# Gated attention and a mixture of experts in one kernel: the early load of the first expert's tokens one slot sooner

## The chip, the cores and the metric

The kernel runs on one core of one Trainium2 chip. A core has five engines, each with an instruction stream of its own that runs strictly in order: TensorE (PE), VectorE (DVE), ScalarE (ACT), GpSimd (POOL) and SyncE (SP), which issues most transfers. The metric is the time on the device in microseconds (us), the median of several runs. The profiled execution has a span of 387.1 us, from its first to its last instruction.

## The reference: what is computed

```python
f = 1.0 / (1.0 + np.exp(-f_logit))                    # B, H, S, D = 4, 8, 768, 48
for t in range(S):                                    # gated linear attention
    state = f[:, :, t, :, None] * state + np.einsum('bhd,bhe->bhde', k[:, :, t], v[:, :, t])
    y[:, :, t] = np.einsum('bhd,bhde->bhe', q[:, :, t], state)
x = y.transpose(0, 2, 1, 3).reshape(3072, 384)        # one row per token
logits = x @ w_gate                                   # 8 experts
expert_idx = np.argmax(logits, axis=1)                # one expert per token
# gate_w: the softmax's value at that expert; each expert takes at most `capacity` tokens, in order
h = np.maximum(disp @ w1, 0.0)                        # (rows, 384) x (384, 1024)
out = gate_w * (h @ w2)                               # (rows, 1024) x (1024, 384), back to the token's row
```

## The kernel before

**Attention** runs in chunks of 128 tokens: 24 chunks (`NT`), 6 to a batch. A loop over `slots`, 0 to 24, writes out by hand the order of the instructions on all five engines; work of neighbouring chunks is interleaved in a slot. In slot n TensorE does, in this order: `keys_pe(n)` (transposes, L443), `scores_pe(n + 1)` (L418), `kq_in(n + 2)` (transposes, L358), `inter(n)` (query times state, L460), `update(n)` (L480), the ranks of a group of tokens (`rank_pe`, L667 to L674), `rows_pe(n - 1)` (the finished token rows, L535) and `values(n)` (L514). Between them stand `early_job(n, 0)`, `early_job(n, 1)` and `early_job(n, 2)`: before `inter`, after it, and after `values`.

**Choice of the expert.** Token rows go into a ring of 12 chunks. For the five groups of chunks that end before chunk 18, `choose_sum`, `choose_max` and `choose_first` find each token's expert on VectorE with help of GpSimd, `rank` and `put` give each token its row in the DRAM buffer `disp`, and the chunks join `queue`. `flush_scatter` takes one chunk from it and stores its 128 rows by index into `disp` (GpSimd, L318). `SCATTERS` says how many are taken in slot n behind `carry(n)` (2 where it has no entry); from slot 20 on `rows_copy` takes one more.

**Weights of the first expert** come in seven pieces (`PIECE_LOAD`: the slot of the load). ScalarE rounds each piece (`split_high`, in the slot of `PIECE_SPLIT`) and a second engine subtracts (`split_low`, L143): VectorE for pieces 3 to 6, GpSimd for pieces 0 to 2, in four parts each. `QUARTERS` gives the slot, the piece and the number of parts there.

**The early part of the first expert.** Its first 256 tokens (`T_FIRST[0]`) are known when chunk 14 is stored (`SPLIT = 15`). One transfer brings them from `disp` to `xg0` (L940). It is issued on SyncE behind slot 20 and waits for the store of chunk 14 (`early_ins`). `early_prep(c)` turns 128 columns of it (two transposes on TensorE, L710, then a rounding on ScalarE, L711, and a subtraction on VectorE, L712), `early_pe(ft)` is one of eight blocks of nine products (L745), and `early_out(ft)` takes a block out of its PSUM bank with one instruction on ScalarE (`hh`, L751) and one on VectorE (`hl`, L752). `EARLY` lists the slot and the place of each. The products of three pools (`psF`, `psT`, `psA`, two banks each) wait for a free bank.

**The experts** follow: `ffn2_rows` for the early tokens, then the rest of expert 0 and the seven others in order of size.

Of the kernel before, what the change touches and what calls it, by code (L numbers as in the profile page):

```python
# [14 lines left out]
ALU = mybir.AluOpType  # L15
# [4 lines left out]
P = 128  # L20
# [8 lines left out]
def kernel(  # L29
# [12 lines left out]
    nc = tc.nc  # L42
    B, H, S, D = q.shape
    N, DM = out.shape
    NE = w_gate.shape[1]
# [5 lines left out]
    NT = B * S // C  # L51
# [20 lines left out]
    PIECE_LOAD = (5, 8, 13, 17, 18, 21, 21)  # L72
    PIECE_SPLIT = (9, 11, 17, 20, 21, 22, 23)
    PARTS = 4
    QUARTERS = {9: (0, 1), 10: (0, 1), 11: (0, 2), 12: (1, 2), 15: (1, 2), 18: (2, 2), 21: (2, 2)}
    SCATTERS = {n: 1 for n in range(NT - 3)}
    PAD_ACT = 7

    const = ctx.enter_context(tc.tile_pool(name="const", bufs=1))
# [24 lines left out]
    def after(ins, other, why):  # L104
        if other is not None:
            tc.add_manual_dep(
                ins.ins,
                other.name,
                mybir.DependencyInfo(mybir.DependencyClass.Sync, mybir.DependencyReason.DATA),
                reason=why,  # L110
            )
# [80 lines left out]
    def load(nm, n):  # L192
        if n >= (NT // 2 if nm == "f" else NT):
            return
        t = loads[nm, n % NLOAD[nm]]
        if nm == "v":
            b, t0 = n // CPB, n % CPB * C
            nc.sync.dma_start(t[:, :, :D], srcs[nm][b, :, t0 : t0 + C, :].rearrange("h p d -> p h d"))
            return
        t = t.rearrange("t h j d -> t h (j d)")  # L200
        if nm == "kq":
            for h, x in enumerate(nm):
                nc.sync.dma_start(t[64 * h : 64 * h + 64], pairs(x, n, C))
        elif n == 0:
            for h, queue in enumerate((nc.sync, nc.scalar)):
                hs = slice(4 * h, 4 * h + 4)
                queue.dma_start(t[:64, hs], pairs(nm, 0, C)[:, hs])
        else:
            nc.sync.dma_start(t, pairs(nm, 2 * n, 2 * C))
# [51 lines left out]
    desc = const.tile([P, NE], F32, name="desc")  # L261
# [301 lines left out]
    def group(g, m):  # L563
        c = g % RING
        return ring_parts[:, c : c + m], rows_at(g, m)[:, :, DM : DM + NE]
# [6 lines left out]
    def choose_max(g, m):  # L572
        part, L = group(g, m)
        most = abuf.tile([P, m], F32, name="r_m")
        nc.vector.tensor_reduce(out=most, in_=L, axis=AX.X, op=ALU.max)
        w = abuf.tile([P, m, NE], F32, name="r_w")
        nc.vector.tensor_tensor(w, L, most.unsqueeze(2).broadcast_to([P, m, NE]), op=ALU.is_equal)
        return w

    def choose_first(g, m, w):  # L580
        nc.gpsimd.tensor_tensor(w, w, desc.unsqueeze(1).broadcast_to([P, m, NE]), op=ALU.mult)
        wm = abuf.tile([P, m], F32, name="r_wm")
        nc.vector.tensor_reduce(out=wm, in_=w, axis=AX.X, op=ALU.max)
        oh = tallies[-1][:, 1 : m + 1]
        nc.vector.tensor_tensor(oh, w, wm.unsqueeze(2).broadcast_to([P, m, NE]), op=ALU.is_equal)
        chosen[g] = oh, m
# [92 lines left out]
    def flush_scatter():  # L679
        if queue:  # L680
            n = queue.pop(0)
            late = n >= SPLIT
            ins = scatter(disp, ri_of.pop(n), row_at(n), NV * RPE - 1, ("disp", "late") if late else ("disp",))
            if not late:
                early_ins[:] = [ins]
# [34 lines left out]
    def early_out(ft):  # L720
        hs0.append(hidden_out(ph0.pop(ft), T_FIRST[0], ft, h0pool, T_FIRST[0]))

    EARLY = {
        (NT - 2, 0): ((early_prep, 0),),
        (NT - 2, 1): ((early_prep, 1),),
        (NT - 2, 2): ((early_prep, 2),),
        (NT - 1, 0): ((early_pe, 0), (early_pe, 1)),
        (NT - 1, 1): ((early_out, 0), (early_pe, 2)),
        (NT - 1, 2): ((early_out, 1), (early_out, 2), (early_pe, 3), (early_pe, 4)),
        (NT, 0): ((early_out, 3), (early_pe, 5)),  # L730
        (NT, 1): ((early_out, 4),),
        (NT, 2): ((early_pe, 6), (early_pe, 7), (early_out, 5), (early_out, 6)),
    }

    def early_job(n, at):
# [81 lines left out]
    def slot(n):  # L817
# [16 lines left out]
        while half:  # L834
            choose_first(*half.pop())
# [45 lines left out]
        if nxt:  # L881
            for s in range(SCATTERS.get(n, 2)):
                flush_scatter()
# [11 lines left out]
        if fn and n >= PAD_ACT:  # L895
            kq_pad(n + 3)
            load("kq", n + 6)
        if n in QUARTERS:
            k, parts = QUARTERS[n]
            for part in range(parts):  # L900
# [9 lines left out]
        while full:  # L910
            g = full.pop()
            half.append((*g, choose_max(*g)))
        if prev and done and not tail:
            g, m = done
# [11 lines left out]
        if tail:  # L926
            early_job(n, 2)
            g, m = done
# [7 lines left out]
                split_low(pieces[k], nc.vector)  # L936
        if n == 4:
            nc.gpsimd.tensor_copy(cap, cap_i[:, 0:1])
        if n == NT - 4:
            ins = nc.sync.dma_start(xg0, dispv[0, : T_FIRST[0]].rearrange("(k p) w -> p k w", p=P))  # L940
            tc.declare_no_dep(ins.ins, group="late", reason="later tokens of this expert go to rows of their own")
            after(ins, early_ins[0], "the rows of the early tokens")
# [72 lines left out]
    with tc.manual_schedule(  # L1015
        engines={
            mybir.EngineType.PE,
            mybir.EngineType.Activation,
            mybir.EngineType.DVE,
            mybir.EngineType.Pool,  # L1020
            mybir.EngineType.SP,
        }
    ):
        prologue()
        for n in slots:
            slot(n)
        while queue:
            flush_scatter()
        early_out(7)
        g0 = gates(xg0, T_FIRST[0] // P, h0pool)  # L1030
# [392 lines left out]
```

## Time and profile before

| | us |
|---|---|
| median of 3 runs | 389.07 |
| lowest and highest | 388.64, 389.6 |
| the profiled execution's own time | 389.2 |
| its span | 387.1 |

The profiled execution lies 0.13 us above the median; 2.1 us of its own time lie outside its span. By the page TensorE is busy for 374.4 us (97%) of the span, VectorE 212.4 (55%), ScalarE 201.4 (52%) and GpSimd 178.5 (46%). A busy time of TensorE says nothing about its pace, since its clock is granted at one of two levels; the clock of a stretch is a column of its own. Times of rows count from the span's start. In the rows a releaser in brackets is what ended the idle time before the instruction.

### The profile page before, as it was taken

To read this page: it belongs to the slowest core of one execution; us is meant where nothing else is said; L and a number is where in the kernel's file an instruction comes from. 1 tells how busy PE (TensorE), PEld (TensorE's weight loads), DVE (VectorE), ACT (ScalarE), POOL (GpSimd) and SP (SyncE) were. 2 spreads that over 40 slices of the span, in tenths; PEclk is the share of its full clock that TensorE was granted. 3 is DMA by queue.
4 is the path that set the end of the run, shared out by engine and by line. 5 is a ranking of instruction groups with operands and counts; after the bars stand their busy time and mean duration, and the time that the engine had idled before them with its cause. 6 is when DMAs were issued, how large, how long until landed. Compare 5 with 4: busy or idle time off the path is not lost.

```text
span 387.1 us, 10152 instructions
## 1 busy us (share of the span) xinstructions
PE 374.4 (97%) x4009; PEld 350.6 (91%) x4009; DVE 212.4 (55%) x490; ACT 201.4 (52%) x425; POOL 178.5 (46%) x263
## 2 busy tenths in 40 slices
PE   8999999999997999999999999999999999999994
PEld 7999888899887789998899989999999999999993
DVE  4998898989989447553844343325235335232310
ACT  3466578877877322462835452544464464462311
POOL 6755546777675832436164340280280271292011
PEclk9999999999999699999999999999999999999999
DMA  8999999999962412669576083165056137211001
GB/s 157 176 207 211 239 251 233 243 225 248 243 154 83 164 68 103 224 206 322 165 253 209 5 270 119 43 218 197 36 179 195 61 108 228 73 58 42 14 23 40
DMA packets 83324, 60.88 MB, mean 157 GB/s; under 512 B 65671, under 2 KB 77829, under 8 KB 83268
## 3 DMA queue, kind: packets, MB, share of 16 engines
q1 hardware_dynamic: 79476, 50.13, 50.3%
q0 software_dynamic: 3520, 9.92, 7.1%
q8 instruction: 33, 0.54, 0.6%
q14 instruction: 23, 0.19, 0.2%
q10 hardware_dynamic: 272, 0.10, 0.1%
HBM read 49.42 MB, written 11.43 MB: 157 GB/s over the span
## 4 chain that ended last, share of the span: by engine, by line
PE 71%; issue 9%; DVE 8%; DMA 4%; POOL 4%; SPq 2%; ACT 1%; POOLq 1%; DVEq 0%
PE psM L1177 14%; PE psA L745 12%; PE psM L745 11%; PE psM L1006 9%; PE psA L418 3%; PE psA L535 3%; PE psY L514 2%; DMA ld_kq<-in_q_dram 2%; PE psT L1148 2%; DVE Rq L392 2%; DVE Suf L378 2%; PE psF L358 2%; PE psY L460 2%; PE psA L368 2%; PE psF L745 2%
## 5 line engine op out<-in xcount | busy, mean ns | idle before, releaser
L318 POOL DMA_INDIRECT out_dram<-yo,g_ti x30 | 30.0, 999 | 101.1 <-ACT yo L1193 40.3
L143 POOL TENSOR_TENSOR w2l<-raw,w2h 128x768 fp32r<-128x768 f32 x28 | 51.1, 1855 | 38.5 <-ACT w2h L134 27.8
L752 DVE SCALAR_TENSOR_TENSOR hl<-psA,hh 128x224 fp32r<-128x224 f32 (+8 forms) x33 | 18.4, 559 | 49.3 <-ACT hh L751 49.3
L143 DVE TENSOR_TENSOR w1l<-raw,w1h 128x1024 fp32r<-128x1024 f32 x21 | 25.4, 1220 | 23.2 <-ACT w1h L134 23.2
L1006 PE MATMUL psM<-w2h,hh 128*128 128x384 f32 (+2 forms) x112 | 37.6, 342 | 0.0
L1006 PE MATMUL psM<-w2l,hh 128*128 128x384 f32 (+2 forms) x112 | 37.5, 338 | 0.0
L1006 PE MATMUL psM<-w2h,hl 128*128 128x384 f32 (+2 forms) x112 | 37.4, 337 | 0.0
L134 ACT ACTIVATE w1h<-raw 128x1024 fp32r<-128x1024 f32 x24 | 25.3, 1062 | 23.1 <-DMA raw<-in_moe_w_dram 23.0
L752 DVE SCALAR_TENSOR_TENSOR hl<-psM,hh 128x224 fp32r<-128x224 f32 (+7 forms) x32 | 17.8, 563 | 31.3 <-ACT hh L751 31.3
L426 POOL TENSOR_SCALAR_AFFINE_SELECT AT<-AT 128x512 f32<-128x512 f32 x48 | 29.7, 643 | 10.1 <-ACT AT L424 9.8
L1177 PE MATMUL psM<-hh,w2h 128*128 128x440 f32 (+3 forms) x96 | 34.1, 355 | 0.0
L1177 PE MATMUL psM<-hl,w2h 128*128 128x440 f32 (+3 forms) x96 | 34.1, 355 | 0.0
L134 ACT ACTIVATE w2h<-raw 128x768 fp32r<-128x768 f32 x32 | 27.1, 846 | 13.3 <-DMA raw<-in_moe_w_dram 12.5
L1177 PE MATMUL psM<-hh,w2l 128*128 128x440 f32 (+3 forms) x96 | 33.8, 352 | 0.0
L318 POOL DMA_INDIRECT disp<-rows,ri x24 | 24.2, 1007 | 17.1 <-DVE tally L645 5.6
L378 DVE TENSOR_TENSOR_SCAN Suf<-psF,direv 112x511 f32<-112x511 f32 x24 | 29.1, 1211 | 4.1 <-PE psF L358 4.1
L751 ACT ACTIVATE hh<-psA 128x224 fp32r<-128x224 f32 (+8 forms) x33 | 16.2, 492 | 26.9 <-PE psA L745 26.2
L745 PE MATMUL psM<-xh,w1h 128*128 128x480 f32 (+6 forms) x84 | 29.8, 354 | 0.0
L745 PE MATMUL psM<-xl,w1h 128*128 128x480 f32 (+6 forms) x84 | 29.8, 354 | 0.0
L745 PE MATMUL psA<-xh,w1h 128*128 128x480 f32 (+6 forms) x84 | 29.7, 353 | 0.0
L745 PE MATMUL psA<-xh,w1l 128*128 128x480 f32 (+6 forms) x84 | 29.5, 351 | 0.0
L392 DVE TENSOR_TENSOR_SCAN Rq<-psF,d 112x512 f32<-112x512 f32 x24 | 29.4, 1224 | 0.0
(238 smaller groups left out, 969.3 us busy)
## 6 DMA issues: line engine op xcount, KB each, us to landing
raw<-in_moe_w_dram SPq DMA_DIRECT2D x24, 512.0 KB, 4.5
raw<-in_moe_w_dram SPq DMA_DIRECT2D x32, 384.0 KB, 3.5
ld_kq<-in_k_dram SPq DMA_DIRECT2D x24, 192.0 KB, 5.4
ld_kq<-in_q_dram SPq DMA_DIRECT2D x24, 192.0 KB, 5.2
ld_v<-in_v_dram SPq DMA_DIRECT2D x24, 192.0 KB, 4.0
ld_f<-in_f_logit_dram SPq DMA_DIRECT2D x11, 384.0 KB, 6.3
xg<-disp SPq DMA_DIRECT2D x6, 589.5 KB, 5.0
xg<-disp SPq DMA_DIRECT2D x3, 393.0 KB
```

The lines of the kernel that those rows point to most:

```text
L134: return nc.scalar.activation(hi, raw, AF.Copy)
L143: engine.tensor_tensor(lo[cs], raw[cs], hi[cs].bitcast(F32), op=ALU.subtract)
L318: ins = nc.gpsimd.indirect_dma_start(out=dst, out_offset=bass.IndirectOffsetOnAxis(ap=idx, axis=0), in_=rows, in_offset=None, bounds_check ...
L378: nc.vector.tensor_tensor_scan(out=_view(Suf[:R], m - 1, [[-1, m]]), data0=_view(F, m, [[-1, m]]), data1=_view(direv[:R], m - 1, [[-1, m]] ...
L392: nc.vector.tensor_tensor_scan(out=Rq[:R], data0=F, data1=d1[:R], initial=0.0, op0=ALU.mult, op1=ALU.max)
L418: nc.tensor.matmul(pas[s][:, p], kTs[n][r, p], qTs[n][r, p], start=True, stop=True)
L426: nc.gpsimd.affine_select(AT[:, s], AT[:, s], pattern=[[0, NP], [1, C]], compare_op=ALU.is_ge, fill=0.0, base=0, channel_multiplier=-1)
L745: nc.tensor.matmul(ph[:, :T], a[:, c, fs], x[:, c, :T], start=(n == 0), stop=(n == 3 * DT - 1))
L751: ins = nc.scalar.activation(hh[:, :T], ph[:, :T], AF.Relu).ins
L752: nc.vector.scalar_tensor_tensor(out=hl[:, :T], in0=ph[:, :T], scalar=0.0, in1=hh[:, :T].bitcast(F32), op0=ALU.max, op1=ALU.subtract)
L1006: nc.tensor.matmul(py[:n], x[:, ks], a[:, ft], start=(ft == 0 and m == 0), stop=(ft == FT - 1 and m == 2))
L1177: nc.tensor.matmul(pys[c][:, :T], a[:, ft, cs], x[:, :T], start=(ft == 0 and n == 0), stop=(ft == FT - 1 and n == 2))
```

## The change

Five things are edited. The transfer into `xg0` is issued behind slot 19 instead of slot 20 (`NT - 5`). `SCATTERS` takes two chunks in slots 18 and 19 and none in slot 20, so that chunk 14 is stored in slot 19. `EARLY` moves the transposes from slot 22 to slots 21, and the blocks of products from slots 23 and 24 to slots 22, 23 and 24. In `choose_max` VectorE multiplies by `desc`, which GpSimd did in `choose_first`. `QUARTERS` moves parts of the subtraction on GpSimd to other slots.

```diff
--- before.py
+++ after.py
@@ -72,8 +72,8 @@
     PIECE_LOAD = (5, 8, 13, 17, 18, 21, 21)
     PIECE_SPLIT = (9, 11, 17, 20, 21, 22, 23)
     PARTS = 4
-    QUARTERS = {9: (0, 1), 10: (0, 1), 11: (0, 2), 12: (1, 2), 15: (1, 2), 18: (2, 2), 21: (2, 2)}
-    SCATTERS = {n: 1 for n in range(NT - 3)}
+    QUARTERS = {11: (0, 3), 12: (0, 1), 15: (1, 3), 17: (1, 1), 20: (2, 2), 21: (2, 2)}
+    SCATTERS = {n: 2 if n in (18, 19) else 0 if n == 20 else 1 for n in range(NT - 3)}
     PAD_ACT = 7
 
     const = ctx.enter_context(tc.tile_pool(name="const", bufs=1))
@@ -575,10 +575,10 @@
         nc.vector.tensor_reduce(out=most, in_=L, axis=AX.X, op=ALU.max)
         w = abuf.tile([P, m, NE], F32, name="r_w")
         nc.vector.tensor_tensor(w, L, most.unsqueeze(2).broadcast_to([P, m, NE]), op=ALU.is_equal)
+        nc.vector.tensor_tensor(w, w, desc.unsqueeze(1).broadcast_to([P, m, NE]), op=ALU.mult)
         return w
 
     def choose_first(g, m, w):
-        nc.gpsimd.tensor_tensor(w, w, desc.unsqueeze(1).broadcast_to([P, m, NE]), op=ALU.mult)
         wm = abuf.tile([P, m], F32, name="r_wm")
         nc.vector.tensor_reduce(out=wm, in_=w, axis=AX.X, op=ALU.max)
         oh = tallies[-1][:, 1 : m + 1]
@@ -721,15 +721,16 @@
         hs0.append(hidden_out(ph0.pop(ft), T_FIRST[0], ft, h0pool, T_FIRST[0]))
 
     EARLY = {
-        (NT - 2, 0): ((early_prep, 0),),
-        (NT - 2, 1): ((early_prep, 1),),
-        (NT - 2, 2): ((early_prep, 2),),
-        (NT - 1, 0): ((early_pe, 0), (early_pe, 1)),
-        (NT - 1, 1): ((early_out, 0), (early_pe, 2)),
-        (NT - 1, 2): ((early_out, 1), (early_out, 2), (early_pe, 3), (early_pe, 4)),
-        (NT, 0): ((early_out, 3), (early_pe, 5)),
-        (NT, 1): ((early_out, 4),),
-        (NT, 2): ((early_pe, 6), (early_pe, 7), (early_out, 5), (early_out, 6)),
+        (NT - 3, 1): ((early_prep, 0),),
+        (NT - 3, 2): ((early_prep, 1), (early_prep, 2)),
+        (NT - 2, 0): ((early_pe, 0), (early_pe, 1)),
+        (NT - 2, 1): ((early_out, 0), (early_out, 1)),
+        (NT - 2, 2): ((early_pe, 2),),
+        (NT - 1, 0): ((early_out, 2), (early_pe, 3)),
+        (NT - 1, 1): ((early_out, 3), (early_pe, 4)),
+        (NT - 1, 2): ((early_out, 4), (early_pe, 5)),
+        (NT, 0): ((early_out, 5),),
+        (NT, 2): ((early_pe, 6), (early_pe, 7), (early_out, 6)),
     }
 
     def early_job(n, at):
@@ -936,7 +937,7 @@
                 split_low(pieces[k], nc.vector)
         if n == 4:
             nc.gpsimd.tensor_copy(cap, cap_i[:, 0:1])
-        if n == NT - 4:
+        if n == NT - 5:
             ins = nc.sync.dma_start(xg0, dispv[0, : T_FIRST[0]].rearrange("(k p) w -> p k w", p=P))
             tc.declare_no_dep(ins.ins, group="late", reason="later tokens of this expert go to rows of their own")
             after(ins, early_ins[0], "the rows of the early tokens")
```

How the instructions stand on TensorE around slots 21 and 22; `xg` is `xg0`, `x0h` and `x0l` are its turned halves, L746 is the old L745. A row with `x2` stands for two instructions.

```order
 L460 MATMUL psY<-qT,S_149 64x128
+L710 MATMUL psF<-ident,xg_85 128x128 x2
 L480 MATMUL psA<-ld_v_112,kn 64x48
...
 L514 MATMUL psY<-AT,ld_v_112 64x128
+L710 MATMUL psF<-ident,xg_85 128x128 x4
 L443 MATMUL psT<-ident,kT 128x64
...
 L418 MATMUL psA<-qT,kT 128x128 x8
-L710 MATMUL psF<-ident,xg_85 128x128 x2
+L746 MATMUL psF<-x0h,w1h 128x256
+L746 MATMUL psF<-x0l,w1h 128x256
```

The first transposes now stand in slot 21 between `inter` and `update`, the other four behind that slot's `values`, and where they stood in slot 22, behind `scores_pe`, two blocks of nine products begin.

GpSimd before, from `carry(19)` (L500) to the subtraction's parts of slot 21:

```order
L500 TENSOR_TENSOR S_147<-U,pendall 112x4x48
L318 DMA disp<-rows,ri 32256x393
L550 COPY rows<-tokid 128x1
L581 TENSOR_TENSOR r_w<-r_w,desc 128x24
L426 AFFINE_SELECT AT<-AT 128x512 x2
L500 TENSOR_TENSOR S_149<-U,pendall 112x4x48
L318 DMA disp<-rows,ri 32256x393
L550 COPY rows<-tokid 128x1
L318 DMA disp<-rows,ri 32256x393
```

And after the change, from the same `carry(19)`:

```order
L500 TENSOR_TENSOR S_147<-U,pendall 112x4x48
L318 DMA disp<-rows,ri 32256x393 x2
L550 COPY rows<-tokid 128x1
L426 AFFINE_SELECT AT<-AT 128x512 x2
L500 TENSOR_TENSOR S_149<-U,pendall 112x4x48
L550 COPY rows<-tokid 128x1
L143 TENSOR_TENSOR w1l<-raw,w1h 128x256 x2
```

Both stores of slot 20 (chunks 13 and 14) stand in slot 19, the product by `desc` (L581) is gone, and two parts of a subtraction stand at the end of slot 20.

SyncE, the last transfers of the attention stage; `ld_v_116` is the load of chunk 23's values, `raw` are the last two weight pieces:

```order
 L198 DMA ld_v_114<-in_v_dram 128x8x48
-L198 DMA ld_v_116<-in_v_dram 128x8x48
-L940 DMA xg_85<-disp 128x2x393
+L941 DMA xg_85<-disp 128x2x393
+L198 DMA ld_v_116<-in_v_dram 128x8x48
 L127 DMA raw<-in_moe_w_dram 128x2x384 x2
```

The transfer into `xg0` has moved ahead of the load of chunk 23's values, which now waits behind it.

## Rows read from the trace of the kernel before

**Rows 1.** The page, part 2: granted TensorE clock in 40 slices, tenths.

```profile
PEclk9999999999999699999999999999999999999999
```

**Rows 2.** Windows, slots 21 to 24: length, busy PE, PEld, DVE, ACT, POOL, clock, DMA share, GB/s.

```profile
117.80:122.41 4.61, 4.61 (x106) 4.19 (x105) 4.58 (x11) 4.00 (x10) 3.88 (x6) 1.00 0.25 89
122.41:126.42 4.01, 1.41 (x25) 1.21 (x24) 3.20 (x15) 2.12 (x6) 0.51 (x1) 1.00 0.48 151
126.42:133.62 7.20, 7.20 (x79) 5.85 (x79) 3.30 (x11) 1.88 (x4) 6.33 (x10) 0.53 0.48 168
133.62:136.10 2.48, 2.48 (x23) 2.27 (x21) 1.92 (x7) 1.94 (x5) 2.05 (x3) 0.99 0.21 81
136.10:140.48 4.38, 3.71 (x58) 3.12 (x58) 1.47 (x8) 1.28 (x5) 2.18 (x4) 1.00 0.38 142
140.48:147.10 6.62, 6.62 (x64) 6.31 (x64) 3.89 (x14) 2.23 (x7) 1.17 (x2) 1.00 0.08 30
```

**Rows 3.** Window, most of the experts' stage, columns as in rows 2.

```profile
175.00:387.00 212.00, 206.39 (x1145) 197.66 (x1143) 75.79 (x156) 95.32 (x171) 75.36 (x58) 1.00 0.40 129
```

**Rows 4.** Chain that ended last, in time, around slot 20: start us, us, what.

```profile
118.06 1.02 POOL disp L318
119.44 3.94 DMA disp<-rows,ri
123.40 2.98 DMA xg<-disp
```

**Rows 5.** Timeline of slot 22: the first transposes of `xg0` on TensorE.

```profile
126.42 0.44 PE L710 MATMUL psF<-ident,xg 128*128 128x128 f32 x2 [2.61 <-DMA xg<-disp]
```

**Rows 6.** Timeline of slot 21: TensorE's groups at full clock.

```profile
119.61 0.67 PE L460 MATMUL psY<-qT,S 48*64 48x128 f32 x16
120.21 0.61 PE L480 MATMUL psA<-ld_v,kn 128*64 128x48 f32 x15
120.71 0.89 PE L535 MATMUL psA<-identc,yT 112*64 112x104 f32 x15
121.36 1.11 PE L514 MATMUL psY<-AT,ld_v 128*48 128x128 f32 x16
122.41 0.46 PE L443 MATMUL psT<-ident,kT 64*128 64x64 f32 x8
```

**Rows 7.** Timeline of slot 23: TensorE's wait for VectorE.

```profile
140.48 0.39 PE L745 MATMUL psF<-x0h,w1h 128*128 128x256 f32 x1 [0.67 <-DVE hl L752]
```

**Rows 8.** Timeline of slot 19: GpSimd's store by index.

```profile
112.62 1.01 POOL L318 DMA_INDIRECT disp<-rows,ri  x1 [0.23 <-issue]
```

**Rows 9.** Line 318, stores by index: issue to landing.

```profile
DMA to landing us min/median/max: 2.4/3.8/6.3
```

**Rows 10.** SyncE's own waits, 95 to 150 us: us in total, times, longest.

```profile
SPq L940 <- DMA disp<-rows,ri: 14.8, 1, 14.8
```

**Rows 11.** Timeline of slot 20: the choice's steps on VectorE and GpSimd.

```profile
114.78 0.23 POOL L581 TENSOR_TENSOR r_w<-r_w,desc 128x24 f32<-128x24 f32 x1 [0.94 <-DVE r_w L577]
115.04 0.18 DVE L583 TENSOR_REDUCE r_wm<-r_w 128x3 f32<-128x24 f32 x1 [0.35 <-POOL r_w L581]
115.12 1.22 POOL L426 TENSOR_SCALAR_AFFINE_SELECT AT<-AT 128x512 f32<-128x512 f32 x2
115.25 0.54 DVE L585 TENSOR_TENSOR tally<-r_w,r_wm 128x24 bf16<-128x24 f32 x1
```

**Rows 12.** Line 583, VectorE: idle before it, us and times.

```profile
  POOL r_w L581: 2.5, 5
```

**Rows 13.** The page, part 6: a weight piece, KB, us from issue to landing.

```profile
raw<-in_moe_w_dram SPq DMA_DIRECT2D x32, 384.0 KB, 3.5
```

**Rows 14.** Line 143 on GpSimd, one part: ns min/median/max, first and last start.

```profile
L143 POOL TENSOR_TENSOR w1l<-raw,w1h x12: 724/734/751, 64.1 to 131.0; 128x256 fp32r<-128x256 f32 x12
```

**Rows 15.** Line 620, VectorE, in slots 22 and 23.

```profile
131.84 1.05 DVE L620 SCALAR_TENSOR_TENSOR r_w<-rows,r_m,desc 128x8 f32<-128x8 f32 x1
139.40 0.23 DVE L620 SCALAR_TENSOR_TENSOR r_w<-rows,r_m,desc 128x8 f32<-128x8 f32 x1
```


## The prediction, made before the changed kernel ran

> **What bounds the kernel now.** I read the granted clock by slices first [rows 1]: TensorE runs at its upper level (2.4 GHz) everywhere except in one slice of 40, the fourteenth. Then the windows by slot around that slice [rows 2]. In each of them TensorE is busy from end to end, except in two: from 122.41 to 126.42 it works 1.41 of 4.01 us, and from 136.10 to 140.48 3.71 of 4.38. The window behind the first gap, 126.42 to 133.62, has a granted clock of 0.53, so the lower level (1.2 GHz), and before and behind it stands 1.00 or 0.99. So the tail of the attention stage loses time twice: TensorE stands, and then it runs at half pace. In the experts' stage it is busy for 206.39 of the last 212.00 us [rows 3]: what reaches that stage sooner ends sooner, as its transfers start from the tail's last stores.
>
> What the gap waits for is in the chain [rows 4]: the store of chunk 14 starts on GpSimd at 119.44 and lands 3.94 later, SyncE then issues the transfer into `xg0` at 123.40, which takes 2.98, and the transposes of slot 22 start at 126.42 after 2.61 us of idle TensorE, released by that transfer [rows 5]. SyncE itself stood 14.8 us before it [rows 10].
>
> **The change, part by part.** I add up what TensorE gains or loses up to the end of slot 24, against the profiled execution's 389.2 us.
>
> *The wait in slot 22 goes:* −2.61 [rows 5], if the tokens are there.
>
> *The low clock goes with it:* what ran from 126.42 to 133.62 in 7.20 us [rows 2] is `inter`, `update`, `rows_pe` and `values` of slots 22 and 21, three pairs of transposes and two groups of rank products. In slot 21 the same four groups start at 119.61, 120.21, 120.71, 121.36 and end where the next slot begins, 122.41: 2.80 us at full clock [rows 6]. A pair of transposes took 0.44 at low clock [rows 5]; I count 0.37 each, 1.1. The rank products are small, I put them at 0.4, an estimate. Together 4.3, so −2.9. The top is everything scaled by the clock, 7.20 × 0.47 = 3.4; the bottom, with transposes at 0.44 and ranks at 0.8, is 2.3.
>
> *The wait in slot 23 goes:* −0.67 [rows 7]. There `early_pe(3)` waited for the VectorE step that frees the bank of `early_pe(1)`. Now `early_out(0)` and `early_out(1)` stand in slot 22 ahead of `update`, and a whole slot lies between. Bounds 0.67 and 0.
>
> *A new wait in slot 21:* `early_prep(0)` now stands behind `inter`, so TensorE asks for `xg0` at 120.21 [rows 6], and `update`, `rows_pe` and `values` are queued behind it. When is it there? The only store of slot 19 started at 112.62 [rows 8]. In the new order two stand there and the second is chunk 14's. The two stores of slot 20 started 1.38 apart with a copy between them [rows 4]; now the copy stands behind both, so I take 1.3: start 113.9, landing 3.94 later at 117.9, transfer 2.98, so 120.9. Cost: +0.7. The bounds come from the range of landings of such stores, 2.4 to 6.3 [rows 9]: there between 119.4 and 123.3, a wait of 0 to 3.1. I take 3.94 because it is the landing of the same store behind the same other store. A wait of 0.67 left the clock at 1.00 in the window behind it [rows 2, 7], so I let 0.7 leave it too.
>
> *The product by `desc` on VectorE:* in slot 20 GpSimd's product starts at 114.78 and VectorE goes on at 115.04, 0.35 idle; a VectorE step of this size takes 0.18 [rows 11]. So some 0.15 a time, five times; the five waits sum to 2.5 [rows 12], with one long one, where GpSimd's copy ahead of the product is what is late. Where VectorE is not on the chain nothing is gained, and the next step (L585, 0.54) runs beside GpSimd's mask as before [rows 11]. I take −0.3; bounds −0.65 and +0.3.
>
> *At nothing:* the eight blocks of products are the same, at full clock in both places (0.99 and 1.00 [rows 2]). The six transposes move. The parts of the subtraction (0.73 each [rows 14]) move by a slot or two on GpSimd; VectorE and TensorE hide them, and `early_pe(0)` in slot 22 needs the first part of piece 2, which stands at the end of slot 20, two us or more ahead. If that cover fails, a part costs its 0.73. On SyncE the load of chunk 23's values now waits behind the transfer, until about 118, and is used in slot 23. Piece 5 comes behind it, and piece 6 waits for GpSimd's last parts in slot 21: `carry(21)` near 123.5, three stores at 1.3, two parts, so about 129, and 3.5 to land [rows 13]. ScalarE wants it in slot 23 at about 131.5 and may stand until 132.5, with `hh` of blocks 2 and 3 behind it. The next to wait would be `early_pe(5)`, whose bank block 2 frees: near 137 by the same walk, so some 2 us of slack are left.
>
> Sum: −2.61 − 2.9 − 0.67 + 0.7 − 0.3 = −5.8. From 389.2 that is 383.4, and as the profiled execution lies 0.13 above the median: **383.3 us**.
>
> **A rule of the skill against it.** GpSimd's mask (L426) starts at 115.12, and the VectorE step L585 that starts beside it at 115.25 takes 0.54 [rows 11]; L620 takes 1.05 in slot 22 and 0.23 in slot 23 [rows 15]. By the Trainium skill (SBUF — State Buffer, Who interferes with whom) a VectorE instruction with two SBUF inputs contends with a GpSimd instruction that reads SBUF, and whichever issues first blocks the other fully; the trace agrees, with 1.05 against 0.23. The moved product has two SBUF inputs, so by that rule it can be blocked where GpSimd could not block itself: the sum would lose up to what rival 2 works out, where by slot 20's rows it loses nothing.
>
> **The rivals.** A measurement tells about 0.3% (1.2 us) from no change.
>
> 1. *The forecast*, 383.3, own range 382 to 385.5: 66%.
> 2. *The moved product is blocked.* It costs 0.82 where a mask or a copy is running (1.05 − 0.23 [rows 15]), at up to four places where VectorE is on the chain: up to 3.3. For it: the two slow rows. Against: in slot 20 the mask only starts at 115.12, behind the product's place, 114.7. Time 384 to 387. 10%.
> 3. *The time saved is partly given back in slots 22 to 24*, where the half clock had hidden chains of VectorE and ScalarE: the choice of one chunk between `rows_pe` and the rank, and piece 6 above. At 0.8 for each of three ranks: 385.7. Against: TensorE has `values` and a block of products ahead of each rank. 9%.
> 4. *The clock falls again in slot 21*, after the wait of 0.7, for as long as it did: 7.2 × 0.47 = 3.4 back, 386.7. Against: the 0.67 of [rows 7]. 6%.
> 5. *The tokens are late*: landing 6.3 [rows 9], a wait of 3.1 and the low clock behind it: −6.5 + 3.1 + 3.4 gives no change, 389.1. The change then only moves the gap to slot 21. 5%.
> 6. *Slower:* the clock falls in slot 21 and does not come back in the sparse slots before the last products: 20 us at 0.53 cost 9.4, 392.7. It decides from some 15 us of low clock (5.8 + 1.2 = 7.0, by 0.47). Against: it came back within 7.2 us as soon as products stood close [rows 2]. 4%.
>
> **How the numbers follow.** Faster: cases 1 to 4, 91%. Same: case 5, 5%. Slower: case 6, 4%. The range goes from 381.9 (all good bounds: −2.61 − 3.4 − 0.67 − 0.65 = −7.3) to 386.8, which takes in cases 2 to 4 and leaves out 5, 6 and the ends, some 17%.
>
> **What would show it.** In the profile after, the first transposes stand in slot 21 at about 120.9 with a wait of 0 to 1.5 released by the transfer; no window from there to the end of slot 24 shows a clock under 0.9; the two blocks of slot 22 begin near 125.5; slot 24's last product ends near 141.5 instead of 147.10; and everything behind keeps its distance. I am wrong if the low clock shows in any slot from 21 on, if the wait in slot 21 is over 2 us, or if the experts' stage shows idle TensorE that it did not have.

## The result, and the profile after

The changed kernel takes **384.2 us** (median of 4 runs, 383.09 to 384.55) where the kernel before takes 389.23 in the runs beside it: a ratio of 0.9867, 95% interval 0.9842 to 0.9893. The forecast was 383.3 with a range of 381.9 to 386.8. The profiled execution has a span of 381.8 and a time of its own of 383.89. Medians and ratios here and below leave out the four executions that took over 1.5% longer than the fastest of their kernel: one of the kernel before at 397.38, one of the filled kernel at 1251.36, two of the one with late tokens at 520.51 and 2014.19.

The page's slices, with the row of TensorE and that of its granted clock, answer to [rows 1]:

```profile
PE   8899999899999999999999999999999999999993
PEclk9999999999999999999999999999999999999998
```

The low slice is gone, and no slice of the tail has a gap. The windows answer to [rows 2, 3]. I cut them at slot starts (the first product of `keys_pe`, L443): slot 20, slot 21, then slots 22 to 24 up to the end of the last early product. First the kernel before, cut in the same way; the columns are those of [rows 2]:

```profile
112.86:117.81 4.95, 4.95 (x111) 4.45 (x111) 4.49 (x13) 4.17 (x11) 2.90 (x6) 1.00 0.12 44
117.81:122.41 4.60, 4.60 (x106) 4.19 (x105) 4.57 (x11) 3.98 (x10) 3.88 (x6) 1.00 0.25 89
122.41:147.36 24.95, 21.67 (x247) 18.99 (x246) 13.83 (x53) 9.45 (x25) 12.23 (x19) 0.86 0.32 114
sum 34.50, PE 31.22 PEld 27.62 DVE 22.89 ACT 17.60 POOL 19.01; mean PE 10.41 PEld 9.21 DVE 7.63 ACT 5.87 POOL 6.34
```

The kernel after:

```profile
113.77:118.73 4.96, 4.96 (x112) 4.46 (x111) 4.79 (x14) 4.18 (x11) 3.64 (x7) 1.00 0.28 93
118.73:124.28 5.55, 5.55 (x113) 4.80 (x111) 5.45 (x14) 4.38 (x12) 4.02 (x7) 1.00 0.63 170
124.28:141.87 17.59, 17.59 (x241) 16.00 (x240) 12.48 (x49) 9.07 (x24) 12.84 (x19) 1.00 0.33 116
sum 28.10, PE 28.10 PEld 25.26 DVE 22.71 ACT 17.63 POOL 20.51; mean PE 9.37 PEld 8.42 DVE 7.57 ACT 5.88 POOL 6.84
```

And what follows the tail up to the end of the span, cut at the same point, before and after:

```profile
147.36:387.10 239.74, 234.03 (x1336) 224.55 (x1333) 92.01 (x225) 107.95 (x198) 85.45 (x67) 1.00 0.42 136
141.87:381.80 239.93, 234.02 (x1337) 224.45 (x1333) 92.14 (x225) 108.12 (x198) 85.36 (x67) 0.99 0.42 136
```

This is the whole gain in one view. The tail took 34.50 us and takes 28.10, 6.40 less. TensorE was busy for 31.22 of the 34.50, so 3.28 were idle: the waits of 2.61 and 0.67 [rows 5, 7]. Now it is busy for all 28.10. The other 3.12 are busy time that shrank, with nearly the same products (464 records before, 466 after): the price of the low clock. Behind the tail TensorE is idle for 5.91 us (239.93 − 234.02) where it was for 5.71 (239.74 − 234.03).

The span is only 5.3 shorter, though, because slot 20 starts at 113.77 and not at 112.86. The timeline of slot 10, first of before, shows where the 0.91 arose (start, length, engine, line, tiles; in brackets the idle time ahead):

```profile
65.71 0.55 PE L480 MATMUL psA<-ld_v,kn 128*64 128x48 f32 x11
66.53 0.32 PE L480 MATMUL psA<-ld_v,kn 128*48 128x48 f32 x5 [0.27 <-issue]
```

and after:

```profile
65.97 0.55 PE L480 MATMUL psA<-ld_v,kn 128*64 128x48 f32 x11
67.76 0.32 PE L480 MATMUL psA<-ld_v,kn 128*48 128x48 f32 x5 [1.23 <-issue]
```

In both TensorE stops behind the eleventh of the 16 products of `update(10)`, and no engine releases it ("issue"): 0.27 and 1.23, 0.96 more. The change moves no instruction of TensorE there, though it takes parts of a subtraction on GpSimd out of slots 9 and 10; the experiments show the stand with and without these edits. So 6.40 less in the tail, 0.91 more ahead of it and 0.19 more behind it (239.74 and 239.93) give the 5.3.

The moved transposes: GpSimd's two stores of slot 19, SyncE's issue, the transfer (its last column is the time to landing) and TensorE in slot 21, from four views. They answer to [rows 4, 5, 6, 8]:

```profile
113.54 1.01 POOL L318 DMA_INDIRECT disp<-rows,ri  x1 [0.23 <-issue]
114.86 0.98 POOL L318 DMA_INDIRECT disp<-rows,ri  x1 [0.30 <-issue]
...
117.93 0.37 SPq L941 DMA_DIRECT2D xg<-disp  x1
...
xg<-disp SPq DMA_DIRECT2D x1, 393.0 KB, 2.9
...
121.13 0.44 PE L710 MATMUL psF<-ident,xg 128*128 128x128 f32 x2
121.49 0.61 PE L480 MATMUL psA<-ld_v,kn 128*64 128x48 f32 x15
```

The second store starts 1.32 behind the first, and the transfer is issued 3.07 later and lands at 120.8. TensorE comes for the tokens at 121.13, and the row has no bracket: no wait.

### The profile page after: what moved, and what is told of

Read it like the earlier page. It is cut to its first block, busy times and chain, and to the rows that moved or that the text cites. A ratio compares the mean times of both kernels' runs of the same rounds, so it can differ in the third digit from the quotient of the medians.

```text
span 381.8 us, 10150 instructions
## 1 busy us (share of the span) xinstructions
PE 370.0 (97%) x4009; PEld 346.8 (91%) x4009; DVE 214.1 (56%) x495; ACT 201.8 (53%) x425; POOL 178.4 (47%) x258
## 5 line engine op out<-in xcount | busy, mean ns | idle before, releaser
L318 POOL DMA_INDIRECT disp<-rows,ri x24 | 25.2, 1049 | 9.9 <-issue 3.9
L746 PE MATMUL psM<-xh,w1h 128*128 128x480 f32 (+6 forms) x84 | 29.7, 354 | 0.0
L746 PE MATMUL psM<-xl,w1h 128*128 128x480 f32 (+6 forms) x84 | 29.7, 354 | 0.0
L746 PE MATMUL psA<-xh,w1h 128*128 128x480 f32 (+6 forms) x84 | 29.7, 353 | 0.0
L746 PE MATMUL psA<-xh,w1l 128*128 128x480 f32 (+6 forms) x84 | 29.4, 350 | 0.0
```

The lines of the kernel that those rows point to most:

```text
L318: ins = nc.gpsimd.indirect_dma_start(out=dst, out_offset=bass.IndirectOffsetOnAxis(ap=idx, axis=0), in_=rows, in_offset=None, bounds_check ...
L746: nc.tensor.matmul(ph[:, :T], a[:, c, fs], x[:, c, :T], start=(n == 0), stop=(n == 3 * DT - 1))
```

## Experiments

They ran in three groups, the first two on one chip and the third on another. The kernel before took 391.47, 391.83 and 391.14 us there, some 2 us more than in the pair above, so each run is compared with the kernel before of its own group. What I take from their traces is the tail (slot 20's start to the last early product) beside the total.

**First group: the parts alone, and the wait filled.** The early load alone is the changed kernel with two edits undone:

```
     QUARTERS as before
-    choose_max:   nc.vector.tensor_tensor(w, w, desc..., op=ALU.mult)
+    choose_first: nc.gpsimd.tensor_tensor(w, w, desc..., op=ALU.mult)
```

> Theory (the early load with its order makes the whole gain): the wait of 2.61, the low clock's 2.9 and the wait of 0.67 go, no wait for xg0 appears, so 383.0 (382.3 to 384.2), no slice with a low clock; if the stand of 1.23 us in slot 10 comes back with it, it belongs to the early load or to chance, if not, to the product or the parts. Rival (product and moved parts are needed, because the early store or piece 2's first part would otherwise be late): a wait of 1 us or more in slot 21 or 22, 385 or more.

386.8 beside 391.47: 0.988 by the medians, and 0.9832 (0.9762 to 0.9902) as the ratio with its interval, wide because the kernel before scattered from 390.5 to 395.45 here. No wait for `xg0`, no low clock, a tail of 29.13 and no stand in slot 10. The rest alone is the opposite: the kernel before with just these two edits made.

```
-    QUARTERS = {9: (0, 1), 10: (0, 1), 11: (0, 2), 12: (1, 2), 15: (1, 2), 18: (2, 2), 21: (2, 2)}
+    QUARTERS = {11: (0, 3), 12: (0, 1), 15: (1, 3), 17: (1, 1), 20: (2, 2), 21: (2, 2)}
-    choose_first: nc.gpsimd.tensor_tensor(w, w, desc..., op=ALU.mult)
+    choose_max:   nc.vector.tensor_tensor(w, w, desc..., op=ALU.mult)
```

> The product on VectorE and the moved parts alone, with the late load of before. Theory: 388.9 (388.3 to 389.5), the wait for xg0 in slot 22 stays at 2.0 to 3.0 us and the low clock behind it stays. Rival 1 (they carry a good part of the gain, as choice and stores come earlier): 387.5 or less, with a wait for xg0 shorter by 1 us or more. Rival 2 (they cost what the head of the changed kernel lost, the stand of TensorE in slot 10): 390 to 390.5, with a stand of about 1.2 us in slot 10.

392.3, a ratio of 0.9998 (0.9964 to 1.0031). The product and the parts carry no gain that this can see. The late tokens were waited for by 0.6 us here and not by the 2.0 to 3.0 expected; the stand in slot 10 was 0.76. And the low clock is missing. Slots 22 to 24:

```profile
127.42:150.94 23.52, 19.93 (x248) 16.96 (x246) 13.20 (x52) 9.34 (x25) 12.17 (x19) 1.00 0.35 121
```

The tail is as long as that of the kernel before above (34.52 and 34.50), at a clock of 1.00: TensorE is idle for 4.25 of it, 1.2 of that before a choice, 1.0 before `hl` and 0.6 before the tokens. So what the long tail consists of differs from execution to execution, and the low clock is a part of it in some.

The changed kernel with one store a slot again:

```
-    SCATTERS = {n: 2 if n in (18, 19) else 0 if n == 20 else 1 for n in range(NT - 3)}
+    SCATTERS = {n: 1 for n in range(NT - 3)}
```

> The changed kernel, but chunk 14's store by index stands in slot 20 again (one store a slot); transposes and products stay early. Theory (the second store in slot 19 is what makes the early transposes free): tokens reach xg0 at about 126, asked for at 121, so a wait of 4 to 6 us in slot 21 and a low clock behind it worth 2 to 3.4 more: 390 to 393, slower than the kernel before. Rival (the clock does not fall there, or the time lost is caught up by the blocks of products moved into slots 22 and 23): 386 to 389, with granted clock over 0.9 in slots 21 and 22.

388.31, a ratio of 0.9895 (0.9860 to 0.9931). The load stayed behind slot 19, where no store of chunk 14 stood ahead of it, so this run leaves out chunk 14's tokens and there was nothing to wait for. It doesn't test the expectation; the second group does.

The kernel before with TensorE kept at work in its wait:

```
+        if n == NT - 2:
+            keep_busy(12)
         early_job(n, 0)
```

> The kernel before, with 12 products of 128x128 whose results nobody reads in TensorE's queue ahead of the late transposes in slot 22, so that TensorE works through its wait of 2.61 us. Theory (the idle stretch is what lowers the clock, and the low clock costs 2.9 by itself): granted clock 0.9 or more in slots 22 and 23, the transposes still start at about 126.4, time 386.3 (385.8 to 387.2). Rival (the clock falls for another reason, or the stretch behind waits for VectorE and ScalarE anyway): 388.5 to 389.8, with the low clock still there or with new waits of 2 us or more in slots 22 to 24.

391.42, a ratio of 0.9982 (0.9946 to 1.0018). The clock stayed up (1.00 in the tail's windows), as it did without a filler in the run with the rest alone, and the time did not move. The two theories are not told apart, as the filler missed its place:

```profile
126.58 1.12 PE L418 MATMUL psA<-qT,kT 48*128 48x128 f32 x16
128.55 2.94 PE L368 MATMUL psA<-ident 128*128 128x128 f32 x24 [0.84 <-ACT AT L424]
131.33 0.38 PE L710 MATMUL psF<-ident,xg 128*128 128x128 f32 x2
```

It waited 0.84 for its own bank, and ran until 131.33, while GpSimd's next store, released by the transfer, shows the tokens there by 128.69. It cost some 2.6 us, about what the clock would have given. And TensorE came for the tokens only at 127.7 in this trace, so the wait to fill was 1 us and not 2.61.

**Second group: late tokens, without and with a filler.** The new order of transposes and products, with chunk 14's store and the load in slot 20 as before:

```
-    SCATTERS = {n: 2 if n in (18, 19) else 0 if n == 20 else 1 for n in range(NT - 3)}
+    SCATTERS = {n: 1 for n in range(NT - 3)}
-        if n == NT - 5:
+        if n == NT - 4:
```

> The changed order of transposes and products, but chunk 14's store and the load of its tokens stand in slot 20 as before. Theory (a wait of some us lowers the clock behind it): TensorE asks for xg0 in slot 21 and waits 3.5 to 6 us, then a stretch of about 7 us with a granted clock near 0.5, and the time is 0.995 to 1.015 of the kernel before, 6 to 9 us above the changed kernel. Rival (the clock does not fall by the wait, or other waits swallow it): granted clock over 0.9 throughout, 3 to 5 us above the changed kernel.

The same with 14 products nobody reads ahead of the transposes in slot 21:

```
+        if n == NT - 3:
+            keep_busy(14)
         early_job(n, 1)
```

> The same as the kernel with late tokens, and 14 products whose results nobody reads stand ahead of the transposes in slot 21, about 3.4 us of work inside the wait. Theory (idle TensorE lowers the clock, and the low clock has a price of its own): granted clock 0.9 or more in slots 21 and 22, the transposes start as late as without the products, and the time is 2 to 3.4 us below the kernel with late tokens. Rival (the low clock costs nothing, as other engines would be waited for at full clock): the clock stays up and the time is within 1 us of the kernel with late tokens.

393.89 and 392.75 beside 391.83: ratios of 1.0064 (1.0040 to 1.0087) and 1.0027 (1.0005 to 1.0049). Windows of the first: slot 21 ahead of the wait, the wait, the stretch up to slot 22, then slot 22's start.

```profile
119.74:123.25 3.51, 3.09 (x58) 2.42 (x56) 3.48 (x8) 2.06 (x6) 3.10 (x5) 1.00 0.27 100
123.30:127.70 4.40, 0.00 (x0) 0.00 (x0) 1.16 (x2) 1.42 (x3) 2.41 (x4) 0.77 0.46 143
127.70:133.05 5.35, 5.34 (x55) 4.52 (x56) 2.00 (x8) 1.08 (x4) 2.55 (x4) 0.55 0.21 80
133.05:136.70 3.65, 3.65 (x43) 3.43 (x42) 3.35 (x5) 2.89 (x9) 3.47 (x5) 1.00 0.32 115
```

The same stretches with the filler:

```profile
119.82:123.60 3.78, 3.13 (x58) 2.42 (x56) 3.75 (x8) 2.33 (x7) 3.37 (x5) 1.00 0.30 109
123.60:127.80 4.20, 3.39 (x28) 3.20 (x28) 0.95 (x2) 1.20 (x2) 2.19 (x4) 1.00 0.45 135
127.80:130.98 3.18, 3.16 (x54) 2.66 (x55) 1.35 (x5) 1.08 (x4) 1.27 (x2) 1.00 0.20 74
130.98:134.60 3.62, 3.62 (x43) 3.43 (x42) 3.33 (x14) 3.10 (x9) 3.13 (x5) 1.00 0.44 122
```

The tokens come at the same moment (127.7 and 127.8), and the same work behind it takes 5.35 us at a granted clock of 0.55 or 3.18 at 1.00: 2.17 less, and by as much the tails differ (35.87 and 33.70). So the clock fell where TensorE stood idle, stayed up where it worked, and the low clock has a price of its own in the tail, beside the wait.

How much of it reaches the end is not settled. The medians differ by 1.14, between the 2 to 3.4 of the theory and the 1 of the rival, and of the two executions in the traces the filled one is the slower (393.59 and 394.45). It takes 2.89 more behind the tail (240.84 and 243.73), where TensorE waits for its next tokens and the clock falls again:

```profile
158.54 0.66 PE L1108 MATMUL psT<-ident,xg 128*128 128x128 f32 x4 [1.83 <-DMA xg<-disp]
```

```profile
160.00:165.00 5.00, 5.00 (x35) 5.00 (x34) 2.17 (x11) 1.17 (x4) 3.30 (x5) 0.71 0.84 279
```

Whether the shorter tail brought that wait about, or chance did, one trace cannot tell. The pair also measures rival 5: with late tokens the new order is slower than the old.

The kernel before once more, for its trace, and the changed kernel beside it:

> The kernel before once more, for its trace on this chip. Theory: the wait for xg0 in slot 22 and the low clock behind it are there again (wait 0.6 to 3 us); the stand in slot 10 after the eleventh product of update is anything between 0 and 1.3 us. Rival (the stand is a part of the change): 0.3 us or less here, and 1 us or more in the changed kernel beside it.

> The changed kernel once more. Theory: 0.984 to 0.989 of the kernel before, no wait of over 1 us for xg0 and no low clock in slots 21 to 24; the stand in slot 10 comes and goes with the moment at which the transfer of instructions begins, so it is another size than 1.23. Rival (the stand belongs to the change): 1.1 to 1.3 us at the same place again.

The changed kernel took 388.16 beside 391.83, a ratio of 0.9899 (0.9871 to 0.9926), just past the 0.984 to 0.989 expected. Three of TensorE's waits in the kernel before, those of 0.7 us or more in its tail (total, times, longest):

```profile
PE psT L674 <- DVE tally L623: 1.2, 1, 1.2
PE psF L710 <- DMA xg<-disp: 0.9, 1, 0.9
PE psF L745 <- DVE hl L752: 0.7, 1, 0.7
```

Here TensorE waits 0.87 for `xg0` and not 2.61, as it comes for it later, and the clock stays at 1.00 behind it. The low stretch comes later, behind two stands of 0.34 and 0.20 and a wait of 1.21 for a choice between 131.7 and 135.3: 0.52 from 135.30 to 138.60.

```profile
128.20:133.60 5.40, 4.69 (x73) 3.36 (x73) 2.47 (x12) 1.93 (x4) 4.66 (x7) 1.00 0.65 229
133.60:135.30 1.70, 0.49 (x6) 0.40 (x6) 1.56 (x8) 1.43 (x5) 1.60 (x3) 0.93 0.01 2
135.30:138.60 3.30, 3.30 (x17) 3.30 (x17) 1.96 (x7) 1.00 (x2) 2.77 (x4) 0.52 0.28 107
```

The changed kernel has no wait for `xg0` and no low clock: its tail is 29.72 against 35.35, 5.63 less. Its profiled run starts slot 20 0.22 later and takes 1.81 more behind the tail (241.32 against 239.51), of which 1.3 is one wait for `hl` in the experts' stage. In neither trace does TensorE stop behind the eleventh product in slot 10 (the 16 products take 0.67 us in the kernel before and 1.00 in the changed one), so the 1.23 is no part of the change.

**Third group: the change step by step.** First the tokens alone (the kernel before with the changed SCATTERS and the load behind slot 19, transposes and products where they were), then the whole early load, then with the parts moved too, then the changed kernel. The edit of the first, against the kernel before; the second adds EARLY of the change, the third QUARTERS, the fourth the product:

```
-    SCATTERS = {n: 1 for n in range(NT - 3)}
+    SCATTERS = {n: 2 if n in (18, 19) else 0 if n == 20 else 1 for n in range(NT - 3)}
-        if n == NT - 4:
+        if n == NT - 5:
```

> The kernel before with only chunk 14's store in slot 19 and the load behind it; transposes and products stay in slots 22 to 24. Theory (the tokens' time is nearly the whole gain, the earlier order adds the wait of 0.67 for hl alone): no wait for xg0, no low clock, 0.67 still there in slot 23, and 0.3 to 1.2 us above the kernel with the whole early load. Rival (the order is needed: with transposes and products still in the last slots TensorE waits there for the choice and the clock falls anyway): a wait of 1 us or more in slots 22 to 24, a low clock behind it, and 2 us or more above the kernel with the whole early load.

> The whole early load (store, load, transposes, products), with the product on GpSimd and the parts where they were before. Theory: 0.985 to 0.990 of the kernel before and within 1 us of the changed kernel. Rival (product and parts together are worth more than their forecast, or cost): 1 us or more from the changed kernel, below it if they cost.

> The changed kernel with the product by desc back on GpSimd. Theory (about 0.15 us a time where VectorE is waited for): 0 to 0.65 us above the changed kernel. Rival (VectorE is blocked there by GpSimd, so that the move costs): 0.5 us or more below the changed kernel.

> The changed kernel beside the three others. Theory: 0.984 to 0.991 of the kernel before, no wait of over 1 us in slots 21 to 24 and no low clock there. Rival (the gain hangs on how late the tokens were on the first chip, 2.61, and is smaller where they are less late): 0.992 or more.

```
                          us      ratio, 95%                tail
before                    391.14
tokens early              389.43  0.9943 (0.9917, 0.9969)   32.40
and the order (EARLY)     386.21  0.9873 (0.9843, 0.9903)   28.92
and the parts (QUARTERS)  386.91  0.9881 (0.9844, 0.9918)   29.62
and the product: changed  387.30  0.9909 (0.9878, 0.9939)   29.59
```

Tokens alone give 1.7, and the order 3.2 more, where I had expected 0.3 to 1.2: the size of the rival, without its low clock. The windows of the two say why (slots 22 to 24, then the sum of slots 20 to 24); the tokens alone:

```profile
125.25:147.24 21.99, 19.52 (x247) 17.07 (x246) 12.96 (x52) 9.55 (x25) 12.49 (x19) 1.00 0.33 108
sum 32.40, PE 29.61 PEld 26.02 DVE 22.07 ACT 17.93 POOL 18.81; mean PE 9.87 PEld 8.67 DVE 7.36 ACT 5.98 POOL 6.27
```

with the order:

```profile
126.23:143.81 17.58, 17.58 (x241) 15.99 (x240) 12.27 (x49) 9.10 (x24) 12.90 (x18) 1.00 0.33 116
sum 28.92, PE 28.60 PEld 25.54 DVE 22.25 ACT 17.87 POOL 19.73; mean PE 9.53 PEld 8.51 DVE 7.42 ACT 5.96 POOL 6.58
```

In the old order 2.47 of slots 22 to 24 are idle, although the tokens are there and the clock is up: 1.17 for `hl`, 0.47 for a choice, 0.54 and 0.19 of "issue". In the trace with the order none of the four is left. The first two are waits that blocks of products now cover. The other two have no releaser, and part of them may be chance, like the stand in slot 10; the rest of the 3.48 by which the tails differ, 1.01, is busy time at the same clock, and no run here explains it.

The last two steps give nothing that can be seen: the medians rise by 0.7 and 0.4, within their intervals. The kernel with the early load alone is 1.1 us below the changed one here, a little more than the 1 expected, and in the first group its medians give 0.988 of the kernel before, where the changed kernel has 0.991 and 0.990. So it has the lowest times of what was run here, but the intervals overlap and the two are not told apart.

One row goes with the longer tail of the last two. ScalarE's copy of the scores in slot 22, with the parts in their old place, and then in the changed kernel:

```profile
128.55 1.09 ACT L424 ACTIVATE AT<-psA 128x512 f32<-128x512 f32 x2 [0.61 <-PE psA L418]
```

```profile
129.76 1.08 ACT L424 ACTIVATE AT<-psA 128x512 f32<-128x512 f32 x2 [2.24 <-PE psF L746]
```

The changed kernel in two groups, and without its product in the third, shows 2.24 to 2.35 us of idle ScalarE at this place, and slot 22 shows `update` waiting 0.22 for that copy in the changed kernel; the two with the parts of before show 0.55 and 0.61. In the trace of the first pair the changed kernel has no such wait. What holds ScalarE there stays open.

## Why the prediction was right, point by point

**The wait in slot 22, −2.61,** went as a whole. Its size is that of one trace and a matter of when TensorE comes: 0.87 in the kernel before on another chip, 0.6 in the run with the rest alone.

**The low clock, −2.9,** measured 3.12 by the busy time of the tail, inside the bounds of 2.3 and 3.4. By groups it is nearer still: what took 7.20 from 126.42 to 133.62 takes 4.21 in the changed kernel, where 4.3 was forecast (3.15 from 127.97 to 131.12, 0.36 and 0.59 for the transposes in slot 21, 0.11 for the second ranks), so 2.99. The pair with and without a filler shows the price apart from the wait, 2.17 for a shorter stretch. But the term belongs to the execution it was read from: the rest alone, with the same late tokens, has no low clock at all.

**The wait in slot 23, −0.67,** was right in the trace compared, and too small as the price of the order. With the tokens alone early, TensorE stands for more than `hl`: 2.47 in slots 22 to 24. The forecast priced the order at 0.67, and it is worth 3.2 us there.

**The new wait in slot 21, +0.7,** was 0, and the mis-sized step is the landing of the store. The tokens came at 120.8 where the forecast had 120.9, but by two misses that cancel: the first store started 0.92 later than in [rows 8], and the second landed in 3.07 and not 3.94. TensorE also came 0.92 later, at 121.13 and not at 120.21: the stand in slot 10 held both back alike, so it did not make the wait go. With a landing of 3.94 the tokens would have come at 121.7 and the wait been some 0.6, an estimate. In all six traces with the early load this landing is 2.7 to 3.4, and none has a wait there.

**The product on VectorE, −0.3,** is not confirmed. The choice of slot 20, its first step before the change, and all of it after, beside [rows 11]:

```profile
114.51 0.18 DVE L577 TENSOR_TENSOR r_w<-rows,r_m 128x24 f32<-128x24 f32 x1
```

```profile
115.42 0.18 DVE L577 TENSOR_TENSOR r_w<-rows,r_m 128x24 f32<-128x24 f32 x1
115.64 0.18 DVE L578 TENSOR_TENSOR r_w<-r_w,desc 128x24 f32<-128x24 f32 x1
115.86 0.18 DVE L583 TENSOR_REDUCE r_wm<-r_w 128x3 f32<-128x24 f32 x1
116.07 0.64 DVE L585 TENSOR_TENSOR tally<-r_w,r_wm 128x24 bf16<-128x24 f32 x1
```

The product took 0.18 and was not blocked. By the Trainium skill (SBUF — State Buffer, Who interferes with whom) a VectorE instruction with two SBUF inputs contends with a GpSimd instruction that reads SBUF, so it could have been. The trace shows it beside a GpSimd store and free, and L585, beside GpSimd's mask, at 0.64 and not 0.54. So 0.35 of waiting became 0.18 of work, 0.10 went to L585, and from the first step's start to the end of L585 the choice takes 1.29 where it took 1.28: nothing gained here. Step by step the median rises by 0.4 with the product, within the intervals. Neither −0.3 nor the bound of +0.3 is shown.

**The rest at nothing** failed at one place that I had not on the list: the head, 0.91 later. It comes from a stand that the kernel before has too (0.27, and none in its second trace) and that is 1.23 in one trace of the changed kernel and none in two others, so in this comparison it is chance, as far as the traces show. Piece 6's load did come late, as walked (ScalarE stood 1.48 in slot 23), and TensorE did not feel it. The sum was then −6.4 in the tail where −5.8 was forecast, and −5.3 in the span: that the total comes so near is partly luck, as a tail 0.6 better met 1.1 lost outside it.

**The signs and the rivals.** The clock is 1.00 in every window from slot 20 to 24, the first block of slot 22 starts at 125.62 and the last early product at 141.59, as forecast. Rivals 2, 4 and 6 did not appear (the moved product takes 0.18 to 0.19 us all five times), 3 at most by the 0.3 to 0.6 of the open wait of ScalarE, and 5 is what the kernel with late tokens shows.

## What to carry to other kernels

Cut the stretch at the same program points in both traces and compare busy time and idle time apart: idle that goes is a wait, busy time that shrinks with the same instructions is the clock. A gap of TensorE in a sparse stretch can cost twice, the wait and a low clock behind it, so an earlier transfer can be worth more than the wait it removes; but compare several executions, since here the low clock came in some and not in others. A move of work into gaps should be priced by all the waits that it covers, not by the one that is longest now. Undo the small edits that travel with a large one: here they bring nothing that can be seen, and the large one alone does as well.

## What the runs showed of the hardware

TensorE stopped in the middle of a run of 16 equal products, always behind the eleventh of `update(10)`, in four of the fourteen traces. In the list of DMA queues one packet of an instruction queue begins shortly before: in the window from 64.8 us in the changed kernel and from 63.8 in the kernel before (packets, MB, share of 16 engines in 0.2 us):

```profile
q8 instruction: 1, 0.02, 42.5%
```

```profile
q8 instruction: 1, 0.02, 35.7%
```

TensorE goes on 2.6 us behind the start of that packet in the kernel before (63.9 and 66.53), 2.9 in the changed one (64.9 and 67.76) and 2.8 and 2.9 in the two other traces with a stand; in those without one it began at least 2.2 us before the eleventh product's end. So the size of the stand follows when that packet gets its turn, which fits a transfer of TensorE's own instructions; that it is these instructions was not tested. By the Trainium skill (Runtime: NRT & Kernel Launch, Instruction fetch mechanics) an engine fetches its instructions in blocks of 16 KiB through a queue of its own, and crossing a block's end is mostly hidden. The packets here have that size (0.02 MB). If they are those blocks, then in these four traces the crossing was not hidden, by 0.27 to 1.23 us.

The low clock did not follow from the waits alone. A wait of 0.87 left 1.00 behind it, one of 1.83 left 0.71 over the 5 us from 160 to 165, one of 4.41 left 0.55, and in the second trace of the kernel before two stands and a wait of 1.21 close together left 0.52, with full-width products running under it for 3.3 us. The rest alone has the same three at the same place (0.32, 0.19 and 1.22), and the same products ran at 1.00 behind them:

```profile
136.49:139.00 2.51, 2.51 (x24) 2.37 (x27) 1.97 (x7) 1.02 (x2) 2.13 (x3) 1.00 0.21 80
```

So these traces give no rule by which a wait could be told to lower the clock or not.
